# The first batch's convolution taps moved into the attention, half of them to GpSimd, and the last result copies to ScalarE

## The chip, the cores and the metric

The kernel runs on one core of a Trainium2 chip. The metric is the device time of one execution in microseconds. The engines are named as the profile names them: PE is TensorE (PEld its weight loads), DVE is VectorE, ACT is ScalarE, POOL is GpSimd, SP is SyncE, which here only issues DMAs. Each engine works through its own instructions in order and waits on semaphores for the others.

## What is computed

Three layers follow each other on 8 batches of 576 rows and 512 columns: a linear attention over 8 heads, a gated convolution, and a Fourier mixer with an MLP.

```
def phi(x):
    proj = np.einsum('bhsd,df->bhsf', x, w_phi)
    proj = proj - np.max(np.abs(proj), axis=-1, keepdims=True)
    return np.concatenate([np.exp(proj), np.exp(-proj)], axis=-1)
x = (q_p @ (k_p^T v)) / (q_p @ sum(k_p) + 1e-6)      # q_p, k_p = phi(q), phi(k); heads side by side
...
for k in range(5):                                   # xp: x with four rows of zeros ahead
    gate_pre += conv_w[k][None, None, :] * xp[:, k:k + S, :]
gate = 1.0 / (1.0 + np.exp(-gate_pre))
x = (gate * (x @ w_val)) @ w_out
...
u = x + real(fft(fft(x, axis=1), axis=2))
un = (u - mean(u)) / sqrt(var(u) + 1e-06)
out = u + maximum(un @ w_ch1, 0) @ w_ch2
```

The change touches the five products and their sum in `gate_pre`, here called taps, for the first batch, and the way in which the attention's result x gets to memory.

## The kernel before

**The attention** runs in 48 steps (and one more to drain), written out by hand in `run_attention`. A unit is two heads of two batches, and three steps make a unit, so the first two batches are done after the first 12 steps and their way through the pipeline. In a step TensorE does, in this order, the numerators (`emit_num`, tile nm), the key-value sums (`emit_KV`, kv), the transpose of a result (`emit_XT`, xt), the transpose of the projected queries (`emit_yT`, yt) and the two projections of the next step (`emit_P`, pj). In the steps whose number 3 divides, kv is split in two, ahead of nm and behind it. VectorE does in a step twice an absolute maximum and a subtraction on a projection (`emit_Y`, tiles m and y), then the copy of the transposed result out of PSUM (`emit_xT`, tile xT), then the scaling of the next result (`emit_X`, tiles r and xs). The transposed result lies in the PSUM bank of the first projection (pj0), so the next step's projection starts only when xT has been copied. ScalarE does the exponentials (ke, qe). SyncE stores xT to x_scr, the attention's result in DRAM, and loads what is needed.

Beside this, ScalarE and GpSimd turn the weights, which come as 64-bit numbers, into pairs of 32-bit ones, in pieces (`convert`, lines 118 to 156): one TENSOR_SCALAR (L143) and three TENSOR_TENSORs (L144, L149, L150) of 1,024 columns each on GpSimd. The pieces are spread over the attention's steps. Tables are loaded and rounded on the way too (`put_table`).

**The mixer and the MLP** are recorded as operations (`op`) with the keys that they read and write, and a planner (`place_ops`) sets their order on all engines by durations and due times. It also chooses between VectorE and GpSimd where an operation allows both (for instance `o_lo`, the low half of a split), and takes it that two operations with both operands in SBUF don't run on these two at once.

For each batch b and each of four blocks m of 128 channels, `note_taps` makes the gate: the fifth product on ScalarE (an activation with a scale), four SCALAR_TENSOR_TENSORs on VectorE that each multiply by a weight and add, and a sigmoid on ScalarE. The running sum lies in a PSUM bank (pa), but for the first two blocks of the first batch in SBUF (sg). `note_V` is the product with w_val (val) and its multiplication with the gate (gv, val, gs), `note_W` the product with w_out (ps). Before the product the batch is split in a high and a low half (xh): for the first batch in the attention's last steps (`split_x`), for the others by `note_x`.

The first batch's rows are loaded (`load_x`) in step 43 (X_AT), into one of two buffers xf, and the four taps of its first block are put into the steps 46 and 47 (`tap_steps`). The other twelve are the planner's, together with the last steps of the attention that are left over (`note_tail`). The layer norm, much later, uses a buffer A of four blocks and a row of sums s1, in a pool of their own (ln).

Of the kernel before, what the change touches and what calls it, by code (L numbers as in the profile page):

```python
# [9 lines left out]
F32 = mybir.dt.float32  # L10
# [6 lines left out]
ALU = mybir.AluOpType  # L17
# [50 lines left out]
def attention_moe_mixer_kernel(  # L68
# [128 lines left out]
    X_AT = TOT - 5  # L197
    att = ExitStack()
# [7 lines left out]
    late["s1"] = ln_p.tile([128, HB], F32, name="s1")  # L206
    late["A"] = ln_p.tile([128, 4, HB], F32, name="A")
# [19 lines left out]
    wp = ap1.tile([128, F], F32, name="wp")  # L227

# [119 lines left out]
    def emit_xT(i):  # L348
# [60 lines left out]
    def put_table(dst, src):  # L409
        r, n = src.shape  # L410
        t = stg.tile([128, 580], F32, tag="tab", name="tab")
        nc.sync.dma_start(out=t[0:r, 0:n], in_=src)
        yield
        hi_act(dst, t[0:r, 0:n])
        yield
# [60 lines left out]
    def load_x(b):  # L476
        t = P["xf"].tile([128, 4, S + 4], F32, tag="xf", name="xf")
        late["xf", b] = t
        nc.vector.memset(t[:, :, 0:4], 0.0)
        nc.sync.dma_start(out=t[:, :, 4:], in_=x_scr[b].rearrange("c p s -> p c s"))  # L480

    def split_x(c):
# [4 lines left out]
        x = late["xf", 0][:, c, 4:]  # L487
# [6 lines left out]
    def tap_steps():  # L494
        t, acc = late["xf", 0], late["sg", 0]
        act.activation(out=acc, in_=shifted(t, 0, 4), func=ACTF.Copy, scale=cw[:, 0, 4:5])
        for k in range(4):
            vec.scalar_tensor_tensor(
                out=acc, in0=shifted(t, 0, k), scalar=cw[:, 0, k:k + 1], in1=acc, op0=ALU.mult, op1=ALU.add
            )  # L500
            yield
# [12 lines left out]
    def note_taps(b, m):  # L514
        t, s = later(("xf", b % 2)), later(("sg", m % 2))
        xk, sk = ("xf", b % 2), ("sg", m % 2)
        first = b == 0 and m < 2
        acc, k = (s, sk) if first else (later("pa")[:, :, 0:HS], "pa")
        if b or m:
# [776 lines left out]
    def note_tail():  # L1296
# [16 lines left out]
        def xt(i):  # L1313
            op("m", 0, lambda e: emit_XT(i, ps_tr, "tr"), [("xs", i % 3), "att"], ["tr"], CH * 0.11)
            op("v", 0, lambda e: emit_xT(i), ["tr"], [("xT", i % 2)], 0.13 + 0.13 * CH)
# [15 lines left out]
    def run_attention():  # L1331
        lead = ((0, 1), (1, 0), (2, 1), (3, 0), (3, 1), (5, 0), (5, 1))
        todo = {}
        tap0 = tap_steps()
# [5 lines left out]
        with tc.manual_schedule():  # L1340
            for st in range(TOT + 1):
# [43 lines left out]
                for _ in range(2 * (TOT - 2 <= st < TOT)):  # L1385
                    next(tap0)
# [3 lines left out]
                if st == X_AT:  # L1390
                    assert did_t == n_t
                    load_x(0)
                    load_x(1)
                    for i in range(2):
                        late["sg", i] = P["g"].tile([128, 2, HS], F32, tag="acc", name="acc")
# [123 lines left out]
```

## Time and profile before

| | us |
|---|---|
| median of 3 runs | 1322.32 (1319.93 to 1325.2) |
| profiled execution, its own time | 1319.91 |
| span of the profiled execution | 1317.9 |
| TensorE busy | 1285.6 |
| VectorE busy | 1150.3 |
| ScalarE busy | 909.0 |
| GpSimd busy | 771.7 |

The busy times are those of the whole span, in which stages with different limits follow each other. A wait is read from the timeline: behind a row stands in brackets how long its engine had been idle before it, and what ended that. Several instructions of a kind that follow each other stand in one row with their count.

### The profile page before, as it was taken

To read this page: it belongs to the slowest core of one execution; us is meant where nothing else is said; L and a number is where in the kernel's file an instruction comes from. 1 tells how busy PE (TensorE), PEld (TensorE's weight loads), DVE (VectorE), ACT (ScalarE), POOL (GpSimd) and SP (SyncE) were. 2 spreads that over 40 slices of the span, in tenths; PEclk is the share of its full clock that TensorE was granted. 3 is DMA by queue.
4 is the path that set the end of the run, shared out by engine and by line. 5 is a ranking of instruction groups with operands and counts; after the bars stand their busy time and mean duration, and the time that the engine had idled before them with its cause. 6 is when DMAs were issued, how large, how long until landed. Compare 5 with 4: busy or idle time off the path is not lost.

```text
span 1317.9 us, 30729 instructions
## 1 busy us (share of the span) xinstructions
PE 1285.6 (98%) x11952; PEld 1183.4 (90%) x11952; DVE 1150.3 (87%) x1790; ACT 909.0 (69%) x1698; POOL 771.7 (59%) x641
## 2 busy tenths in 40 slices
PE   8999999988999998999999999999999999999998
PEld 7899999977999998998888888888888888889997
DVE  6888888879999999789989989998989888888885
ACT  6888898654556646466867687767677676776662
POOL 4877778224567576264655755596558856583321
PEclk9999999999999999999999999999999999999999
DMA  8689999624343442428433753357333733355322
GB/s 307 205 282 302 297 302 298 193 73 141 117 165 104 165 153 100 146 79 284 132 103 98 227 155 103 104 159 217 105 103 119 238 122 100 104 153 177 105 85 89
DMA packets 147005, 214.62 MB, mean 163 GB/s; under 512 B 18854, under 2 KB 105382, under 8 KB 146860
## 3 DMA queue, kind: packets, MB, share of 16 engines
q1 hardware_dynamic: 142400, 203.06, 47.9%
q10 hardware_dynamic: 4460, 9.62, 2.0%
q8 instruction: 93, 1.52, 0.5%
q14 instruction: 52, 0.43, 0.1%
HBM read 165.63 MB, written 46.99 MB: 161 GB/s over the span
## 4 chain that ended last, share of the span: by engine, by line
PE 89%; DVE 5%; ACT 3%; DMA 1%; issue 1%; SPq 0%; POOL 0%; DVEq 0%; POOLq 0%
PE cx L64 15%; PE x L64 15%; PE ps L64 13%; PE cy L64 11%; PE y L64 8%; PE val L64 7%; PE kv L64 5%; PE pj L64 5%; PE nm L64 4%; PE z L64 4%; PE yt L307 2%; PE xt L345 1%; DVE acc L64 1%; ACT qe L64 1%; DMA r<-s_scr 1%
## 5 line engine op out<-in xcount | busy, mean ns | idle before, releaser
L64 POOL TENSOR_TENSOR r<-r 128x256 fp32r<-128x256 f32 (+1 forms) x301 | 292.7, 989 | 246.5 <-ACT r L64 233.3
L64 ACT ACTIVATE r<-r 128x256 fp32r<-128x256 f32 (+1 forms) x420 | 195.3, 487 | 54.9 <-DMA r<-s_scr 49.9
L64 PE MATMUL x<-un,r 128*128 128x462 f32 (+1 forms) x960 | 221.7, 372 | 2.2 <-ACT c L64 1.4
L64 PE MATMUL cx<-h,r 128*128 128x462 f32 (+1 forms) x960 | 213.9, 371 | 1.1 <-DVE acc L64 1.1
L64 PEld LDWEIGHTS x<-un,r 128*128 128x128 f32 x960 | 180.3, 188 | 23.9 <-DVE c L64 2.0
L64 PEld LDWEIGHTS cx<-h,r 128*128 128x128 f32 x960 | 180.3, 188 | 22.1 <-DVE acc L64 1.9
L64 PE MATMUL cy<-h,r 128*128 128x462 f32 (+1 forms) x720 | 160.2, 371 | 0.0
L64 PEld LDWEIGHTS cy<-h,r 128*128 128x128 f32 x720 | 135.4, 188 | 15.3
L64 PE MATMUL val<-xh,wv 128*128 128x290 f32 x768 | 117.1, 301 | 7.5 <-DVE gs L64 3.8
L64 PEld LDWEIGHTS val<-xh,wv 128*128 128x128 f32 x768 | 107.8, 191 | 10.2 <-DVE gs L64 4.5
L64 PE MATMUL y<-un,r 128*128 128x462 f32 (+1 forms) x480 | 113.9, 372 | 0.7 <-DVE h L64 0.6
L64 DVE SCALAR_TENSOR_TENSOR acc<-xf,cw,acc 128x576 f32<-128x576 f32 x128 | 105.9, 830 | 6.9 <-ACT acc L64 5.9
L64 PE MATMUL ps<-ge,wo 128*128 128x290 f32 x768 | 107.9, 297 | 2.0 <-DVE A L64 1.8
L64 PEld LDWEIGHTS ps<-ge,wo 128*128 128x128 f32 x768 | 104.6, 189 | 2.6 <-DVE A L64 2.1
L266 DVE TENSOR_REDUCE m<-pj 128x6 f32<-128x768 f32 x96 | 91.5, 953 | 15.6 <-PE pj L64 14.2
L64 PEld LDWEIGHTS y<-un,r 128*128 128x128 f32 x480 | 90.0, 188 | 11.9 <-DVE h L64 1.5
L64 DVE TENSOR_TENSOR acc<-cx,acc 128x924 f32<-128x924 f32 (+1 forms) x80 | 89.0, 1112 | 12.6 <-PE cx L64 10.5
L267 DVE TENSOR_TENSOR y<-pj,m 128x768 f32<-128x768 f32 x96 | 92.0, 958 | 6.4
L64 ACT ACTIVATE qe<-yt 128x768 f32<-128x768 f32 x96 | 72.5, 808 | 27.4 <-PE yt L307 27.4
L64 PE MATMUL kv<-vraw,ke 128*64 128x66 f32 x2560 | 88.3, 224 | 1.9 <-ACT kvT L64 1.8
L64 PE MATMUL pj<-wp,kqraw 64*128 64x128 f32 x1152 | 81.9, 290 | 6.9 <-DMA kqraw<-in_k_dram 4.8
L64 PEld LDWEIGHTS pj<-wp,kqraw 64*128 64x128 f32 x1152 | 71.9, 196 | 18.2 <-DVE xT L64 11.1
(170 smaller groups left out, 2719.3 us busy)
## 6 DMA issues: line engine op xcount, KB each, us to landing
r<-s_scr SPq DMA_DIRECT2D x280, 128.0 KB, 2.3
r<-s_scr SPq DMA_DIRECT2D x140, 256.0 KB, 2.6
raw<-in_w_ch_dram SPq DMA_DIRECT2D x32, 512.0 KB, 6.1
vraw<-in_v_dram SPq DMA_DIRECT2D x32, 330.0 KB, 5.7
xf<-x_scr SPq DMA_DIRECT2D x8, 1152.0 KB, 6.7
u_scr<-u ACTq DMA_DIRECT2D x8, 1152.0 KB, 5.3
kqraw<-in_k_dram SPq DMA_DIRECT2D x46, 192.0 KB, 3.7
kqraw<-in_q_dram SPq DMA_DIRECT2D x46, 192.0 KB, 4.0
```

Source lines behind the costliest of these rows:

```text
L64: return lambda *a, **k: f(*(resolve(x) for x in a), **{n: resolve(x) for n, x in k.items()})
L266: nc.vector.tensor_reduce(out=m, in_=pv, axis=AX.X, op=ALU.max, apply_absolute_value=True)
L267: nc.vector.tensor_tensor(out=y, in0=pv, in1=m.unsqueeze(3).to_broadcast([128, 2, CH, F]), op=ALU.subtract)
L307: nc.tensor.transpose(t[:, h, j * F:(j + 1) * F], y[:, h, j, :], ident)
L345: nc.tensor.transpose(t[:, 0, j * F:(j + 1) * F], x[:, j].rearrange("p h d -> p (h d)"), ident)
```

## The change

The fifth product and the four others of all four blocks of the first batch are now done in the attention. The rows of the first batch are loaded in step 19 instead of 43, into a buffer of its own, x0, which lies where the layer norm's A and s1 lie (these are now views of x0). Both xf buffers stay free for the batches that follow.

GpSimd makes the fifth product of all four blocks (`tap_start`, two blocks at the end of step 20, two at the end of step 28) and, for the blocks 0 and 1, the other taps in halves of 288 columns, as a product and a sum (`tap_steps_pool`): eight pairs between the steps 21 and 35, eight in the steps 42 to 45. VectorE makes the four taps each of the blocks 2 and 3 (`tap_steps_dve`), one in each of the steps 21, 24, 27 to 42, with the sum in a new SBUF tile tp. The taps of the steps 46 and 47, and the first batch's in the planner's part, are gone; only the sigmoids are left there.

The copies xT run on ScalarE from step 42 on and in the part that is left over (eleven of 48). The tables are staged in a tile of another pool.

```
+    x0 = ln_p.tile([128, 4, S + 4], F32, name="x0")
+    late["A"] = flat0[:, 0:4 * HB].rearrange("p (c s) -> p c s", s=HB)
+    late["s1"] = flat0[:, 4 * HB:5 * HB]
...
+    tp = ap1.tile([128, 2, 2, HS], F32, name="tp")
...
-        vec.tensor_copy(out=xT[i], in_=t[:, 0, 0:CH * F])
+        (hi_dve if e == "v" else hi_act)(xT[i], t[:, 0, 0:CH * F])
...
+    def tap_start(m):
+        acc = late["sg", m] if m < 2 else tp[:, m - 2]
+        gps.tensor_scalar(out=acc, in0=shifted(x0, m, 4), scalar1=cw[:, m, 4:5], scalar2=None, op0=ALU.mult)
+
+    def tap_steps_pool():
+        for m in range(2):
+            acc = late["sg", m]
+            for k in range(4):
+                for a in range(2):
+                    t = P["g"].tile([128, NE], F32, tag="gv", name="tap")[:, 0:HS]
+                    gps.tensor_scalar(out=t, in0=shifted(x0, m, k)[:, a], scalar1=cw[:, m, k:k + 1], scalar2=None, op0=ALU.mult)
+                    gps.tensor_tensor(out=acc[:, a], in0=acc[:, a], in1=t, op=ALU.add)
+                    yield
+
+    def tap_steps_dve():
+        for m in range(2, 4):
+            acc = tp[:, m - 2]
+            for k in range(4):
+                vec.scalar_tensor_tensor(
+                    out=acc, in0=shifted(x0, m, k), scalar=cw[:, m, k:k + 1], in1=acc, op0=ALU.mult, op1=ALU.add
+                )
+                yield
...
+            op("a", 128 * CH, lambda e: emit_xT(i, "a"), ["tr"], [("xT", i % 2)])
...
+                if X_FIRST + 2 <= st <= X_FIRST + 23 and st % NG == 0:
+                    next(tap_d)
                 if at(5):
                     emit_XT(st - 5, ps_pj, "pj0")
-                    emit_xT(st - 5)
+                    emit_xT(st - 5, "v" if st < X_AT - 1 else "a")
...
-                for _ in range(2 * (TOT - 2 <= st < TOT)):
-                    next(tap0)
+                if st == X_FIRST:
...
+                    load_x(0)
+                for i in range(2):
+                    if st == X_FIRST + 1 + 8 * i:
+                        tap_start(i)
+                        tap_start(i + 2)
+                if X_FIRST + 2 <= st < X_FIRST + 18 and (st - X_FIRST) % 2 == 0:
+                    next(tap_p)
+                if X_AT - 1 <= st < X_AT + 3:
+                    next(tap_p)
+                    next(tap_p)
```

What stands on VectorE in step 21, from the second projection on. Before (m and y are the maximum and the subtraction, xT the copy of the result, r and xs its scaling):

```order
L266 TENSOR_REDUCE m<-pj 128x6
L267 TENSOR_TENSOR y<-pj,m 128x768
L64 COPY xT<-xt 128x384
L335 TENSOR_SCALAR r<-nm 128x6
L336 RECIPROCAL r<-r 128x6
L337 TENSOR_TENSOR xs<-nm,r 128x384
```

And now (x_114 is x0):

```order
L270 TENSOR_REDUCE m<-pj 128x6
L271 TENSOR_TENSOR y<-pj,m 128x768
L64 SCALAR_TENSOR_TENSOR tp<-x_114,cw,tp 128x576
L64 COPY xT<-xt 128x384
L339 TENSOR_SCALAR r<-nm 128x6
L340 RECIPROCAL r<-r 128x6
L341 TENSOR_TENSOR xs<-nm,r 128x384
```

The tap stands between the subtraction and the copy; so it does in the six other steps 24 to 39.

What stands on GpSimd around the end of step 20. Before (mt is the piece of weights in the making, raw its 64-bit numbers, cv a temporary):

```order
L143 TENSOR_SCALAR mt<-raw_2066 128x1024
L144 TENSOR_TENSOR mt<-mt,cv 128x1024
L149 TENSOR_TENSOR mt<-mt,raw_2066 128x1024
L150 TENSOR_TENSOR mt<-mt,cv 128x1024
L143 TENSOR_SCALAR mt<-raw_2176 128x1024
```

And now (acc is the sum of block 0, tp that of block 2, cw the convolution's weights):

```order
L143 TENSOR_SCALAR mt<-raw_2066 128x1024
L144 TENSOR_TENSOR mt<-mt,cv 128x1024
L64 TENSOR_SCALAR acc<-x_114,cw 128x576
L64 TENSOR_SCALAR tp<-x_114,cw 128x576
L149 TENSOR_TENSOR mt<-mt,raw_2066 128x1024
L150 TENSOR_TENSOR mt<-mt,cv 128x1024
L143 TENSOR_SCALAR mt<-raw_2176 128x1024
L144 TENSOR_TENSOR mt<-mt,cv 128x1024
L64 TENSOR_SCALAR tap<-x_114,cw 128x288
L64 TENSOR_TENSOR acc<-acc,tap 128x288
```

The two first products stand behind the second of the four instructions of a piece, and the first pair of halves behind the second instruction of the next piece.

What stands on VectorE where the attention ends, from the scaling of step 46 on. Before:

```order
L337 TENSOR_TENSOR xs<-nm,r 128x384
L64 SCALAR_TENSOR_TENSOR acc<-xf,cw,acc 128x576 x2
L266 TENSOR_REDUCE m<-pj 128x6
L267 TENSOR_TENSOR y<-pj,m 128x768
L266 TENSOR_REDUCE m<-pj 128x6
L267 TENSOR_TENSOR y<-pj,m 128x768
L64 COPY xT<-xt 128x384
L335 TENSOR_SCALAR r<-nm 128x6
```

And now, to the first gate of the first batch (val is the product with w_val):

```order
L341 TENSOR_TENSOR xs<-nm,r 128x384
L270 TENSOR_REDUCE m<-pj 128x6
L271 TENSOR_TENSOR y<-pj,m 128x768
L339 TENSOR_SCALAR r<-nm 128x6
L340 RECIPROCAL r<-r 128x6
L341 TENSOR_TENSOR xs<-nm,r 128x384
L64 SCALAR_TENSOR_TENSOR acc<-xf,cw,acc 128x2x288 x4
L64 TENSOR_TENSOR gv<-val_5453,acc 128x290
L64 TENSOR_TENSOR val_5456<-val_5456,acc 128x290
```

Taps and copies are out of these steps; the four taps ahead of the first gate are those of the second batch.

## Rows read from the trace of the kernel before

**Rows 1.** The page: busy time, share of the span, instructions of each engine.

```profile
PE 1285.6 (98%) x11952; PEld 1183.4 (90%) x11952; DVE 1150.3 (87%) x1790; ACT 909.0 (69%) x1698; POOL 771.7 (59%) x641
```

**Rows 2.** By stage: window, length, busy PE PEld DVE ACT POOL, clock, DMA, GB/s.

```profile
100.00:120.00 20.00, 20.00 (x488) 18.66 (x485) 17.79 (x27) 17.98 (x23) 16.45 (x9) 1.00 0.89 290
273.00:296.00 23.00, 17.94 (x351) 16.41 (x348) 16.89 (x26) 11.68 (x19) 4.11 (x4) 0.93 0.16 51
296.00:330.00 34.00, 28.95 (x306) 27.22 (x306) 32.10 (x63) 14.86 (x22) 14.40 (x20) 0.95 0.41 137
488.00:510.00 22.00, 16.92 (x120) 15.94 (x119) 20.05 (x36) 13.16 (x24) 10.99 (x11) 1.00 0.28 102
```

**Rows 3.** Timeline, TensorE in steps 46 and 47: start, us, engine, line, what, idle before.

```profile
274.35 1.61 PE L64 MATMUL pj<-wp,kqraw 64*128 64x128 f32 x24
...
281.31 0.52 PE L345 MATMUL xt<-ident,xs 128*128 128x128 f32 x3 [2.40 <-DVE y L267]
...
283.54 2.93 PE L64 MATMUL pj<-wp,kqraw 64*128 64x128 f32 x24 [1.05 <-DVE xT L64]
```

**Rows 4.** Timeline, TensorE's waits for VectorE in the first batch.

```profile
301.24 1.87 PE L64 MATMUL val<-xh,wv 128*128 128x290 f32 x12 [1.04 <-DVE gv L64]
309.83 1.62 PE L64 MATMUL nm<-kvT,qe 128*64 128x65 f32 x48 [1.08 <-DVE xs L337]
316.16 1.87 PE L64 MATMUL val<-xh,wv 128*128 128x290 f32 x12 [0.95 <-DVE gs L64]
321.13 4.56 PE L64 MATMUL val<-xh,wv 128*128 128x290 f32 x20 [1.22 <-DVE xh L64]
```

**Rows 5.** Timeline, step 21 and the load that stands ahead of it.

```profile
118.86 0.52 SPq L412 DMA_DIRECT2D tab<-in_feat_tab_dram  x1
...
124.89 2.39 POOL L144 TENSOR_TENSOR mt<-mt,cv 128x1024 int32<-128x1024 int32 x1
...
124.98 0.96 DVE L267 TENSOR_TENSOR y<-pj,m 128x768 f32<-128x768 f32 x1
...
126.62 0.56 DVE L64 COPY xT<-xt 128x384 f32<-128x384 f32 x1 [0.68 <-PE xt L345]
...
127.23 0.86 PEld L64 LDWEIGHTS pj<-wp,kqraw 64*128 64x128 f32 x14 [0.23 <-DVE xT L64]
...
127.36 2.40 POOL L149 TENSOR_TENSOR mt<-mt,raw 128x1024 int32<-128x1024 int32 x1
```

**Rows 6.** Timeline, taps on VectorE beside GpSimd: sum in SBUF, then in PSUM.

```profile
277.21 1.48 POOL L64 TENSOR_TENSOR xh<-xf,xh 128x576 fp32r<-128x576 f32 x1 [3.55 <-ACT xh L64]
...
277.45 1.86 DVE L64 SCALAR_TENSOR_TENSOR acc<-xf,cw,acc 128x576 f32<-128x576 f32 x1
...
305.91 3.21 POOL L64 TENSOR_TENSOR ws<-ws 128x256 f32<-128x256 f32 x4 [6.43 <-DMA ws<-s_scr]
...
306.37 0.82 DVE L64 SCALAR_TENSOR_TENSOR acc<-xf,cw,acc 128x576 f32<-128x576 f32 x1
```

**Rows 7.** Groups on GpSimd, 20 to 262 us: count, busy us, mean ns, idle before.

```profile
L149 POOL TENSOR_TENSOR mt<-mt,raw 128x1024 int32<-128x1024 int32 x20 | 48.4, 2419 | 6.7 <-ACT raw L146 5.9
...
L143 POOL TENSOR_SCALAR mt<-raw 128x1024 int32<-128x1024 uint16 x19 | 22.3, 1174 | 26.0 <-DMA s_scr<-mt 22.0 <-DMA x_scr<-xT 2.5 <-DMA raw<-in_w_ch_dram 1.0
```

**Rows 8.** Timeline, subtractions and running conversions in the steps 27 and 39.

```profile
160.57 0.96 DVE L267 TENSOR_TENSOR y<-pj,m 128x768 f32<-128x768 f32 x1
...
160.61 2.37 POOL L150 TENSOR_TENSOR mt<-mt,cv 128x1024 int32<-128x1024 int32 x1
...
230.16 2.38 POOL L144 TENSOR_TENSOR mt<-mt,cv 128x1024 int32<-128x1024 int32 x1
...
230.97 0.96 DVE L267 TENSOR_TENSOR y<-pj,m 128x768 f32<-128x768 f32 x1
```

**Rows 9.** The page, DMA issues: KB each, us to landing.

```profile
xf<-x_scr SPq DMA_DIRECT2D x8, 1152.0 KB, 6.7
```

**Rows 10.** Timeline, TensorE behind its longest wait in the mixer.

```profile
506.85 1.87 PE L64 MATMUL val<-xh,wv 128*128 128x290 f32 x12 [2.89 <-DVE gs L64]
```

More of the change, by code (lines that the diff above doesn't have):

```diff
@@ L205, in attention_moe_mixer_kernel @@
     ln_p = pool(lx, "ln", 1, side=R)
-    late["s1"] = ln_p.tile([128, HB], F32, name="s1")
-    late["A"] = ln_p.tile([128, 4, HB], F32, name="A")
+    x0 = ln_p.tile([128, 4, S + 4], F32, name="x0")
+    flat0 = x0.rearrange("p c s -> p (c s)")
+    late["A"] = flat0[:, 0:4 * HB].rearrange("p (c s) -> p c s", s=HB)
+    late["s1"] = flat0[:, 4 * HB:5 * HB]
     wv_p = pool(gx, "wv", 1, side=R)
@@ L410, in put_table @@
         r, n = src.shape
-        t = stg.tile([128, 580], F32, tag="tab", name="tab")
+        t = P["g"].tile([128, 2, NE], F32, tag="gs", name="tab").rearrange("p a b -> p (a b)")
         nc.sync.dma_start(out=t[0:r, 0:n], in_=src)
@@ L476, in load_x @@
     def load_x(b):
-        t = P["xf"].tile([128, 4, S + 4], F32, tag="xf", name="xf")
-        late["xf", b] = t
-        nc.vector.memset(t[:, :, 0:4], 0.0)
+        t = late["xf", b] if b else x0
         nc.sync.dma_start(out=t[:, :, 4:], in_=x_scr[b].rearrange("c p s -> p c s"))
@@ L486, in split_x @@
         h, l = late["xh", 0], late["xh", 1]
-        x = late["xf", 0][:, c, 4:]
+        x = x0[:, c, 4:]
         hi_act(h[:, c], x)
@@ L492, in shifted @@
         return t[:, m, k:k + S].rearrange("p (a s) -> p a s", a=2)
[L494 to L501, printed above, removed]
+    def tap_start(m):
[18 more added lines that the diff above has]
+                yield
     def note_x(b):
@@ L516, in note_taps @@
         xk, sk = ("xf", b % 2), ("sg", m % 2)
-        first = b == 0 and m < 2
-        acc, k = (s, sk) if first else (later("pa")[:, :, 0:HS], "pa")
-        if b or m:
+        if b:
+            acc, k = later("pa")[:, :, 0:HS], "pa"
+        else:
+            acc, k = (s, sk) if m < 2 else (tp[:, m - 2], "att")
+        if b:
             o_act(acc, shifted(t, m, 4), ACTF.Copy, 685, [xk], [k], scale=cw[:, m, 4:5])
@@ L1384, in run_attention @@
                     next(c)
-                for _ in range(2 * (TOT - 2 <= st < TOT)):
-                    next(tap0)
+                if st == X_FIRST:
+                    for i in range(2):
+                        late["sg", i] = P["g"].tile([128, 2, HS], F32, tag="acc", name="acc")
+                    nc.vector.memset(x0[:, :, 0:4], 0.0)
+                    load_x(0)
+                for i in range(2):
+                    if st == X_FIRST + 1 + 8 * i:
[6 more added lines that the diff above has]
+                    next(tap_p)
                 while did_t < n_t and did_t * (X_AT - 5) < (st - 3) * n_t:
@@ L1391, in run_attention @@
                     assert did_t == n_t
-                    load_x(0)
+                    for b in range(2):
+                        late["xf", b] = P["xf"].tile([128, 4, S + 4], F32, tag="xf", name="xf")
+                        nc.vector.memset(late["xf", b][:, :, 0:4], 0.0)
                     load_x(1)
-                    for i in range(2):
-                        late["sg", i] = P["g"].tile([128, 2, HS], F32, tag="acc", name="acc")
                 if st in (X_AT + 2, X_AT + 3):
```

6 lines of the change are left out of this document (3 added, 3 removed).

## The prediction

> **What bounds the kernel now.** I read the busy shares first: TensorE is busy for 98% of the span, so only its idle or slowed stretches can be won [rows 1]. The table by stage shows where these are [rows 2]. In the attention TensorE is full (20.00 of 20), VectorE has 17.79 and GpSimd 16.45. From 273 to 330, where the attention hands over to the first batch of the mixer, TensorE loses 5.06 us (23 - 17.94) and then 5.05 us (34 - 28.95), with a granted clock of 0.93 and 0.95, while VectorE has 32.10 of 34 in the second part. A second hole lies at 488 to 510 (22 - 16.92 = 5.08 us).
>
> The timeline at 277 to 284 names the cause of the first part: TensorE's transpose waits 2.40 us for VectorE, the next projection another 1.05 us, and its 24 matmuls then take 2.93 us against 1.61 two steps before [rows 3]. In front of those VectorE rows stand convolution taps of the first batch. In the second part waits for VectorE of 1.04, 1.08 and 0.95 us, all on gates, row scalings or sums queued among taps, and a last one of 1.22 us for the split of the next batch [rows 4]. The change works on exactly this place: 16 taps at some 0.82 us and eleven copies at 0.56 us leave VectorE there.
>
> The steps that receive the taps are then what to look at. In step 21 (all steps with a number that 3 divides look like it) VectorE finishes the second subtraction at 125.94, sits idle for 0.68 us, copies xT until 127.18, and TensorE's projection starts at 127.23, as soon as xT is out of its bank [rows 5]. So in a TensorE that is full, the copy xT is on the path with no slack behind it, and what VectorE has in front of it is 0.68 us (0.77 with the overlap of the two instructions).
>
> **The change part by part.**
>
> Eight taps on VectorE in the attention. Each is put between that subtraction and xT [rows 5]. A tap needs 0.82 us, 0.73 until the next may start, so without any hindrance it just fits into the gap: about 0.05 us a tap. But it reads two operands from SBUF, and so do the conversions of GpSimd. At 277.45 such a tap took 1.86 us: GpSimd's split had begun at 277.21 and ended at 278.69, and the tap's own work came behind that. With its sum in PSUM a tap at 306.37 took 0.82 beside a GpSimd busy with sums of the weights from 305.91 to 309.12 [rows 6]. The new sums (tp) lie in SBUF, so each tap waits for what is left of the running conversion. Price: each piece of weights is three TENSOR_TENSORs of 2.4 us, of which rows 7 show one, and a TENSOR_SCALAR of 1.17 us; some 60 and 19 of them in 242 us [rows 7] leave a mean rest of (60 x 2.4 x 2.4 + 19 x 1.17 x 1.17) / (2 x 242) = 0.77 us at a moment of no relation to them. At the six places where the taps 2 to 7 go, the trace of before has for instance 1.5 us left in step 27 (160.61 + 2.37 against 161.53 less the overlap of 0.09) and 0.7 in step 39 [rows 8]. The least is nothing, the most a whole conversion, 2.4 us. I take 0.8 each: six taps, **+5 us**, with 0 and 14 as ends. TensorE has no idle time with which to make this up.
>
> The first tap is dearer. Its sum is begun by GpSimd, and the order puts these two instructions behind the conversion that ends at 127.28 in the trace [rows 5]. They also need the batch's rows: that load is issued where the table load at 118.86 stands [rows 5]; alike loads land after 6.7 us (125.6) [rows 9], and in an attention that moves 290 GB/s [rows 2] the 1.18 MB can take 4.1 us longer (129.6). I take 127.8. Two TENSOR_SCALARs of 576 columns, at most 1.17 us each by the 1,024 columns of rows 7 and 0.66 by their share, 0.7 taken, end at 129.2; the tap ends by 130.0, and xT, before at 126.62, starts 3.4 us late. If the conversion that follows on GpSimd (2.40 us, row at 127.36) begins before the tap does, it is 5.8. No row shows this race; I take 4.6. A TensorE idle so long may lose its clock: 1.32 us were lost behind 2.40 + 1.05 us [rows 3], nothing behind 2.89 us (twelve matmuls in 1.87, as at 316.16) [rows 4, 10]. I count 1.3, so **+6 us**, ends 3.4 and 8.
>
> The eighth tap, in step 42, meets no conversion and no xT on VectorE: nothing.
>
> The other half on GpSimd: 4 first products and 16 pairs of product and sum. By rows 7 a pair costs up to 288/1024 of 1.17 and 2.42, or 1.0 us, some 19 us in all. Eight pairs lie among conversions, which leave GpSimd 3.5 of 20 us [rows 2]; nobody but the stores waits for a conversion at once, and if they came so late that ScalarE waited, its exponentials would. Eight lie behind the last conversion, where GpSimd has nothing. Zero, with that cover.
>
> Here a rule speaks against the change. Beside VectorE's subtraction at 124.98, which reads PSUM, GpSimd's conversion from 124.89 costs it nothing: 0.96 us [rows 5]. The Trainium skill (Perfetto Trace Analysis, Optimizing Scalar/DVE Operations) warns that the two share a read port of SBUF, so that moving work from one to the other may not help. By the row only VectorE's own eight taps meet that port, and the sum below stands; by the rule more of GpSimd's added work comes back as waits of VectorE, and the time would be that of the first rival.
>
> What else moves: the load of the first batch goes past 24 steps of SyncE's queue. The loads behind it land up to 4.1 us later once; the keys and queries of a unit are asked for six steps ahead, and values and weights have a step or more, so nothing; if a piece of weights were late, ScalarE, which reads it first, would stand for some us. The small clearing of x0 on VectorE and the tables' other tile: nothing. A and s1 as views of x0 are first written when the first batch is long done: nothing.
>
> Copies on ScalarE: eleven copies of 384 columns. In the last steps ScalarE waits for the transpose behind it anyway, and the copy takes its place in the same gap; nothing, or up to 0.5 us a copy (0.56 on VectorE, rows 5) if exponentials stand in front of it.
>
> What is won: the whole of 2.40 + 1.05 + 1.32 = 4.8 us at the attention's end [rows 3], since no tap and no copy is left in VectorE's steps there. Of the next 35 us, 1.04 + 1.08 + 0.95 = 3.1 us [rows 4]; the taps of the next batch, four in a row, come before the first gate, where VectorE would be idle. At 321.13 20 matmuls took 4.56 us where 12 take 1.87, 1.4 us too long, behind a wait of 1.22 us [rows 4]. That wait is for splits of the next batch that one buffer holds back, and stays in kind; I count 1.2 of the 2.6. **-9 us**, ends 5 and 11. What is late next is that split.
>
> The rest of the mixer gets another order from the planner, and gives five more splits to VectorE, so that little of its relief is left at 488. I count nothing, and 3 us either way. From the MLP on TensorE's order is as before.
>
> Sum: 5 + 6 - 9 = **+2 us** on a profiled execution of 1319.91 us (its span of 1317.9 and 2.0 around it), which lies 2.4 us under the median of the three runs; on the median, 1322.3 + 2 = **1324 us**.
>
> **The rivals.**
>
> Slower: GpSimd's conversions own VectorE's taps. If the first tap loses the race and the clock (8 us), the six others wait 1.5 us each instead of 0.8 (9 us), and only 7.5 us are won, it is +9.5: **1332 us**. For it speaks that GpSimd gets more work in those steps, so fewer gaps; against it the rests read at the places, which are smaller. It decides from 1.3 us a tap on (8 + 8 - 9 = +7).
>
> Faster: the relief of VectorE reaches the hole at 488 to 510. There a gate's sums came 2.89 us late [rows 10], with VectorE at 20.05 of 22 [rows 2]. If these 5 us go too, the first tap costs 4 and the others 0.5 each, it is 4 + 3 - 9 - 5 = -7: **1315 us**. Against it: TensorE runs ahead by as much as VectorE is relieved.
>
> The change does not do what it says: the first batch is held by the split and by the sigmoids on ScalarE behind a table load, and only the 4.8 us at the attention's end come: 11 - 5 = +6, **1328 us**.
>
> **How the numbers follow.** Chances: the forecast 0.55, slower 0.2, faster 0.15, not done 0.1. A measurement of this kernel can tell about 0.5%, 6.6 us, from no change. The forecast's own range is 1319 to 1330. Of the faster case most lies beyond 6.6 us, and a little of the forecast's lower end; of the slower case most, with a part of the last: faster 0.18, same 0.59, slower 0.23. The range, with a tenth left out on either side, is 1314 to 1333.
>
> **What the profile would show.** Right: in step 21 an idle TensorE of 3 to 6 us ended by xT; in steps 24 to 39 a tap of 0.8 to 3 us and a projection late by as much over 0.7; no wait of TensorE for VectorE at the attention's end; steps there at 5.7 and 6.2 us. Wrong: taps at 0.82 us in all steps (then some 5 us faster), a first tap that finds its sum ready, or waits of TensorE for ScalarE's copies.

## The result, and the profile after

The changed kernel takes 1327.36 us in the median of 7 runs (1324.96 to 1332.06); the kernel before, beside it, 1319.21 us (7 runs). The ratio is 1.0056, 95% interval 1.0034 to 1.0077: slower by some 7 to 8 us. The forecast was +2 us (1324 on a median of 1322.3); the time lies in the range 1314 to 1333, and the difference is 5 to 6 us larger than forecast. The prediction gave 0.59 to no change and 0.23 to a slowdown beyond 6.6 us, the least that it took a measurement to tell; the 7 to 8 us lie just beyond that.

First the page of the changed kernel, busy time, share and instructions of each engine; it answers to [rows 1].

```profile
PE 1286.3 (97%) x11952; PEld 1182.4 (89%) x11952; DVE 1144.8 (86%) x1775; ACT 909.9 (69%) x1705; POOL 802.5 (61%) x674
```

TensorE does the same work in a longer span (1325.4 us in the profiled execution, 1317.9 before). GpSimd has 30.8 us more. Where the time lies shows in the table by stage (window, length, busy PE PEld DVE ACT POOL, clock, DMA, GB/s), beside [rows 2]:

```profile
100.00:120.00 20.00, 20.00 (x472) 18.66 (x467) 17.59 (x29) 17.48 (x22) 16.82 (x9) 1.00 0.90 291
120.00:140.00 20.00, 11.58 (x213) 10.70 (x213) 12.30 (x17) 11.15 (x14) 12.39 (x7) 0.77 0.68 238
287.20:305.20 18.00, 16.40 (x353) 15.05 (x348) 10.48 (x18) 12.04 (x20) 3.51 (x3) 1.00 0.26 80
305.20:340.00 34.80, 32.99 (x347) 31.26 (x346) 29.18 (x61) 18.17 (x30) 12.86 (x14) 1.00 0.31 111
340.00:498.00 158.00, 153.53 (x1137) 149.89 (x1136) 146.40 (x276) 87.54 (x180) 93.70 (x91) 1.00 0.42 143
498.00:520.00 22.00, 20.63 (x154) 20.00 (x154) 20.97 (x39) 15.93 (x36) 14.09 (x14) 1.00 0.32 121
```

One new hole of 8.42 us (20 - 11.58) with a clock of 0.77 stands at 120 to 140. The end of the attention and the first batch now lose 1.60 and 1.81 us at full clock, where 5.06 and 5.05 us were lost. The hole at 488 to 510 has shrunk to 1.37 us, but 4.47 us are lost in the 158 us ahead of it, where the kernel before lost 0.36:

```profile
330.00:488.00 158.00, 157.64 (x1185) 156.36 (x1184) 150.84 (x282) 92.62 (x188) 103.92 (x92) 1.00 0.41 142
```

The waits of TensorE in the changed kernel (120 to 600 us; total, times, longest):

```profile
PE pj L64 <- DVE xT L64: 12.5, 6, 8.4
PE val L64 <- DVE gv L64: 3.6, 5, 1.0
PE yt L311 <- ACT qe L64: 1.6, 1, 1.6
PE ps L64 <- POOL f L64: 1.1, 2, 0.6
PE val L64 <- DVE gs L64: 1.0, 4, 0.4
PE xt L349 <- ACT xT L64: 0.9, 1, 0.9
```

Six waits for xT, one of them 8.4 us long, stand behind the six taps out of eight that a conversion of GpSimd held up. To follow this step by step I compare the start of TensorE's transpose xt in both timelines (us):

| start of | before | after | later by | change since the line above |
|---|---|---|---|---|
| xt, step 21 | 126.04 | 125.37 | -0.67 | -0.67 |
| xt, step 22 | 132.25 | 142.31 | 10.06 | +10.73 (first tap) |
| xt, step 40 | 237.71 | 252.50 | 14.79 | +4.73 (six taps) |
| xt, step 48 | 290.03 | 299.18 | 9.15 | -5.64 (attention's end) |
| the MLP's first product | 596.82 | 604.13 | 7.31 | -1.84 (handover, mixer) |
| end of the span | 1317.94 | 1325.44 | 7.50 | +0.19 |

The timeline of the changed kernel in step 21 shows the first tap; it answers to [rows 5]:

```profile
118.19 0.65 SPq L482 DMA_DIRECT2D x<-x_scr  x1
...
124.04 2.39 POOL L144 TENSOR_TENSOR mt<-mt,cv 128x1024 int32<-128x1024 int32 x1
...
128.08 1.73 POOL L64 TENSOR_SCALAR acc<-x,cw 128x576 f32<-128x576 f32 x1 [1.65 <-DMA x<-x_scr]
129.79 1.73 POOL L64 TENSOR_SCALAR tp<-x,cw 128x576 f32<-128x576 f32 x1
...
131.48 2.38 POOL L149 TENSOR_TENSOR mt<-mt,raw 128x1024 int32<-128x1024 int32 x1
131.55 2.92 DVE L64 SCALAR_TENSOR_TENSOR tp<-x,cw,tp 128x576 f32<-128x576 f32 x1 [6.27 <-POOL tp L64]
...
134.40 0.54 DVE L64 COPY xT<-xt 128x384 f32<-128x384 f32 x1
...
134.99 2.93 PE L64 MATMUL pj<-wp,kqraw 64*128 64x128 f32 x24 [8.42 <-DVE xT L64]
...
137.86 2.87 PE L64 MATMUL nm<-kvT,qe 128*64 128x65 f32 x48
140.51 1.87 PE L64 MATMUL kv<-vraw,ke 128*64 128x66 f32 x48
```

The rows land at 128.08, the two products take 1.73 us each, and the next conversion begins 0.07 us ahead of the tap, which then ends 0.61 us behind it. The copy xT starts 8.45 us late (134.40 against 126.62 - 0.67). The rest is the clock: in the windows 134.99 to 137.86 and 137.86 to 140.70 the granted clock is 0.50, that is 1.2 of 2.4 GHz, and TensorE's next three groups take 2.93, 2.87 and 1.87 us where 1.61, 1.62 and 1.57 are usual, 2.87 us more. Of the 10.73 us only 2.28 are left for it, because in the kernel before this step had itself lost 0.53 us (6.22 us from xt to xt; an undisturbed one takes 5.69).

At the attention's end the rows that answer to [rows 3] and [rows 4] have no wait left above 0.9 us (one of 1.60 us, of the transpose yt for ScalarE's qe, stands in step 48 of both kernels):

```profile
293.05 0.55 PE L349 MATMUL xt<-ident,xs 128*128 128x128 f32 x3
...
294.22 1.61 PE L64 MATMUL pj<-wp,kqraw 64*128 64x128 f32 x24
...
307.76 1.62 PE L64 MATMUL nm<-kvT,qe 128*64 128x65 f32 x48
...
310.94 2.68 PE L64 MATMUL val<-xh,wv 128*128 128x290 f32 x18 [0.35 <-DVE gs L64]
...
325.43 0.55 PE L349 MATMUL xt<-ident,xs 128*128 128x128 f32 x3 [0.89 <-ACT xT L64]
...
327.08 4.71 PE L64 MATMUL val<-xh,wv 128*128 128x290 f32 x30 [0.30 <-DVE gs L64]
```

### The profile page after: what moved, and what is told of

Same layout as the page of the kernel before. It is cut to its first block, busy times and chain, and to the rows that moved or that the text cites. A ratio compares the mean times of both kernels' runs of the same rounds, so it can differ in the third digit from the quotient of the medians.

```text
span 1325.4 us, 30762 instructions
## 1 busy us (share of the span) xinstructions
PE 1286.3 (97%) x11952; PEld 1182.4 (89%) x11952; DVE 1144.8 (86%) x1775; ACT 909.9 (69%) x1705; POOL 802.5 (61%) x674
## 4 chain that ended last, share of the span: by engine, by line
PE 81%; DVE 8%; ACT 5%; DMA 3%; POOL 2%; issue 2%; SPq 0%; DVEq 0%; POOLq 0%; ACTq 0%
PE cx L64 14%; PE x L64 14%; PE cy L64 11%; PE ps L64 10%; PE y L64 8%; PE pj L64 5%; PE val L64 4%; PE kv L64 4%; PE nm L64 4%; PE z L64 4%; DVE acc L64 2%; PE yt L311 2%; PE xt L349 1%; DVE m L270 1%; DMA r<-s_scr 1%
## 5 line engine op out<-in xcount | busy, mean ns | idle before, releaser
L64 DVE SCALAR_TENSOR_TENSOR acc<-xf,cw,acc 128x576 f32<-128x576 f32 x112 | 91.2, 814 | 11.6 <-ACT acc L64 11.0
L64 PE MATMUL pj<-wp,kqraw 64*128 64x128 f32 x1152 | 82.3, 291 | 17.2 <-DVE xT L64 12.5
```

Of the source, the lines that this page charges most:

```text
L64: return lambda *a, **k: f(*(resolve(x) for x in a), **{n: resolve(x) for n, x in k.items()})
```

## The experiments

All times in this table are from the runs; the last five columns are from the one profiled execution of each and say by how much TensorE took longer than in the profiled execution before, in the stretches of the table above.

| kernel | median, us | before, same chip | ratio (95%) | 21 to 22 | 22 to 40 | 40 to 48 | 48 to MLP | MLP |
|---|---|---|---|---|---|---|---|---|
| changed | 1327.36 | 1319.21 | 1.0056 (1.0034 to 1.0077) | 10.73 | 4.73 | -5.64 | -1.84 | 0.2 |
| e1_late3 | 1320.52 | 1322.10 | 0.9987 (0.9971 to 1.0003) | -0.53 | 7.80 | -5.64 | -1.62 | 1.4 |
| e7_first | 1324.52 | 1320.35 | 1.0018 (1.0000 to 1.0036) | 5.02 | 4.61 | -5.64 | -0.93 | 3.2 |
| e2_psum | 1316.58 | 1322.10 | 0.9958 (0.9942 to 0.9973) | -0.53 | 3.98 | -5.64 | -0.78 | -0.5 |
| e3_act_xT | 1319.05 | 1322.10 | 0.9977 (0.9959 to 0.9996) | -0.53 | 3.52 | -5.59 | -1.59 | 0.2 |
| e10_vector_half | 1319.11 | 1321.18 | 0.9983 (0.9967 to 0.9999) | 0.20 | 4.28 | -5.64 | -2.33 | -0.2 |
| e4_no_taps | 1314.09 | 1322.10 | 0.9939 (0.9916 to 0.9962) | -0.53 | 2.50 | -5.64 | -1.79 | -0.4 |
| e11_no_taps2 | 1314.53 | 1321.45 | 0.9952 (0.9938 to 0.9967) | -0.20 | 1.24 | -5.64 | -1.48 | 3.4 |
| e9_gpsimd_half | 1317.12 | 1321.18 | 0.9968 (0.9950 to 0.9986) | -0.53 | 2.70 | -5.64 | -1.32 | -0.3 |
| e12_gpsimd2 | 1316.52 | 1321.45 | 0.9966 (0.9951 to 0.9981) | -0.53 | 3.12 | -5.64 | -2.02 | 4.1 |
| e8_late_load | 1315.34 | 1320.35 | 0.9948 (0.9929 to 0.9967) | -0.07 | 1.08 | -5.60 | -1.56 | 1.3 |
| e6_copies | 1319.16 | 1320.35 | 0.9984 (0.9967 to 1.0001) | -0.53 | 1.19 | -1.51 | -0.34 | 0.8 |
| e5_end | 1315.49 | 1320.35 | 0.9956 (0.9939 to 0.9973) | 0.29 | 1.07 | -5.64 | -1.50 | 3.9 |

Some columns need a caution. In the first, -0.53 is an undisturbed step, since the kernel before lost 0.53 us there. e6_copies does in the steps 21 to 40 what the kernel before does, and still shows 1.19 there; e5_end and e8_late_load show 1.1 too. So some 1.1 us in that column is an execution's own; e4_no_taps, without any tap, shows 2.50. And the MLP, which no edit touches, differs by up to 4 us from one execution to the other, so what the trace alone shows is worth that much, and I go by the medians first. The profiled execution is also not always a middle one: that of e9_gpsimd_half is its fastest (1313.25 us), that of e5_end its slowest (1318.73).

The kernel before took 1319.21 us beside the changed kernel and 1320.35 to 1322.10 beside the others. Most times named in the expectations are on the former, so kernels of different chips are compared by their ratios.

**The first tap.** e1_late3 takes it away, e7_first makes it cheaper.

```diff
-                if X_FIRST + 2 <= st <= X_FIRST + 23 and st % NG == 0:
+                if X_FIRST + 5 <= st <= X_FIRST + 26 and st % NG == 0:
                     next(tap_d)
```

> The changed kernel with VectorE's eight taps one unit later (steps 24 to 45 in place of 21 to 42), nothing else moved. Six of them still stand ahead of the copy xT, in the same six steps; only the tap whose sum GpSimd has just begun is gone. Theory: in the changed kernel this first tap alone cost TensorE 10.7 us (8.4 us of waiting and 2.3 us at a lower clock), and nothing gives it back, so 1327.4 - 10.7 = 1316.7 us (1315 to 1319), with TensorE's start of step 22 where it was before the change. Rival: the stall belongs to the early load and to GpSimd's own delay, and comes again at another wait: 1324 to 1328.

Against the changed kernel the ratio falls by 0.0069, 9.1 us. The median of 1320.52 us lies over the theory's 1315 to 1319, but the kernel before is 2.9 us slower there too, and by the ratio the time is 1317.5 on the first measurement's before. The delay of step 22 is gone, whole, and doesn't come again: the theory holds, and with it goes more than the whole loss. By itself the kernel is at most 0.3% from before (the interval holds 1). Its steps 24 to 39 were dearer than the changed kernel's, since other taps met other conversions and TensorE once waited for kvT; both are taken up below.

```diff
-                if st == X_FIRST:
+                if st == X_FIRST - 2:
                     nc.vector.memset(x0[:, :, 0:4], 0.0)
                     load_x(0)
...
-                        tap_start(i)
                         tap_start(i + 2)
+                        tap_start(i)
```

> The changed kernel with the first tap made cheaper, nothing else moved: the load of the first batch in step 17 in place of 19, and GpSimd begins block 2, which VectorE needs, ahead of block 0 (and block 3 ahead of block 1). Theory: the delay of TensorE at step 22, 10.7 us, was 1.65 us for the load, 1.73 us for each of two first products, 2.2 us for the tap that lost against the next conversion, 2.3 us of slow clock, and the step's own. Now the load is there, one product stands in front of the tap, and the instruction that gets in ahead of it is a product of 1.73 us in place of 2.38: a delay of 5.5 to 7 us, and a time 3.5 to 5 us under the changed kernel's. Rival: the tap finds its operands only when the conversion behind is over as well, so that only the load is won: 1.7 us.

Step 22 is 5.02 us late in place of 10.73, and the ratio lies 0.0038 (5.0 us) under the changed kernel's. The tap waits for one product only, and no conversion gets in ahead of it, but the product of block 0: it takes 1.30 us. The slow clock is still there behind a wait of 4.04 us (24 matmuls in 2.93 us), but the next 48 take 1.80 where they took 2.87. The delay is 0.5 us under the theory's 5.5 to 7, the time at the end of its 3.5 to 5, so the parts are right to about that much.

**The six taps behind it.** e2_psum takes away the second operand in SBUF, e3_act_xT the copy behind the tap, e10_vector_half GpSimd's added work; the first two stand on e1_late3.

```diff
+        late["pj"] = pv.rearrange("p h c f -> p h (c f)")[:, :, 0:HS]
...
-                    out=acc, in0=shifted(x0, m, k), scalar=cw[:, m, k:k + 1], in1=acc, op0=ALU.mult, op1=ALU.add
+                    out=acc, in0=shifted(x0, m, k), scalar=cw[:, m, k:k + 1], in1=late["pj"], op0=ALU.mult, op1=ALU.add
```

> As e1_late3, but each of VectorE's taps reads as its second operand a piece of the projection in PSUM that it has just subtracted, in place of the running sum in SBUF (the sum of blocks 2 and 3 is left out). Number, place and size of the instructions stay. Theory (a VectorE instruction with two operands in SBUF waits for GpSimd's running conversion): taps of 0.82 us, the six steps 24 to 39 lose at most 0.3 us in place of 4.7, so e1_late3 less 4.5 us, about 1312. Rival (the tap's own length ahead of xT is what costs): TensorE's delay over the six steps stays at 3 to 5 us, and the time is that of e1_late3.

A tap beside a conversion in the timeline of e1_late3:

```profile
235.03 2.37 POOL L144 TENSOR_TENSOR mt<-mt,cv 128x1024 int32<-128x1024 int32 x1
235.09 2.94 DVE L64 SCALAR_TENSOR_TENSOR tp<-x,cw,tp 128x576 f32<-128x576 f32 x1
...
237.49 2.79 POOL L149 TENSOR_TENSOR mt<-mt,raw 128x1024 int32<-128x1024 int32 x1
...
238.55 2.68 PE L64 MATMUL pj<-wp,kqraw 64*128 64x128 f32 x24 [2.08 <-DVE xT L64]
```

And one beside the same kind of conversion in the timeline of e2_psum:

```profile
217.37 2.41 POOL L149 TENSOR_TENSOR mt<-mt,raw 128x1024 int32<-128x1024 int32 x1
218.10 0.80 DVE L64 SCALAR_TENSOR_TENSOR tp<-x,cw,pj 128x576 f32<-128x576 f32 x1
```

All eight taps of e2_psum take 0.80 or 0.81 us, and no wait for xT is left; the time falls by 0.0029 (3.8 us). In e1_late3 two taps of 2.80 and 2.94 us began 0.17 and 0.06 us after a conversion had begun and cost 1.95 and 3.65 us, the second with the clock. That a tap with two operands in SBUF waits for GpSimd is shown. The Trainium skill (SBUF — State Buffer, "Who interferes with whom") says it in the same way: a VectorE instruction with two inputs in SBUF contends with a GpSimd instruction that reads SBUF, because its second input comes through a read interface that the two share, and the shared pair of ports is an exclusive lock. The trace agrees: the tap of 2.94 us ends 0.62 us behind the conversion. That the six steps would lose at most 0.3 us did not hold: e2_psum still loses 3.7 us in the steps 32 to 34, by another wait, of TensorE for kvT, told with GpSimd's half.

```diff
-                    emit_xT(st - 5, "v" if st < X_AT - 1 else "a")
+                    emit_xT(st - 5, "v" if st < X_AT - 1 and not (st >= X_FIRST + 5 and st % NG == 0) else "a")
```

> As e1_late3, but in the six steps 24 to 39 with a tap the copy xT runs on ScalarE, so that no tap stands ahead of it. Theory (a tap costs because it is ahead of xT, whatever makes it long): the six steps cost at most 1 us in place of 4.7, so about 1312 to 1314. Rival: ScalarE stands in an activation of 1.2 us of the conversions when the transposes end, so that xT starts up to 1.2 us late there, 4 to 7 us over six steps: 1316 to 1319.

By the trace the theory holds: taps of 1.29 and 1.66 us stand there without a wait of TensorE for VectorE, and 22 to 40 fell from 7.80 to 3.52. What is left is one wait for kvT (1.2) and two of 0.69 us for ScalarE's xT, in the steps 24 and 33; there ScalarE stands in an activation of 1.26 and 1.23 us of the conversions, the rival's cause, but in two steps of six. By the medians the kernel is only 0.0010 (1.3 us) under e1_late3, within the spread, and its 1319.05 us, or 1316.2 on the first before, is nearer to the rival's 1316 to 1319 than to the theory's 1312 to 1314. So the medians don't decide, and how much of these 4 us is to be had in every execution stays open.

```diff
-        gps.tensor_scalar(out=acc, in0=shifted(x0, m, 4), scalar1=cw[:, m, 4:5], scalar2=None, op0=ALU.mult)
+        act.activation(out=acc, in_=shifted(x0, m, 4), func=ACTF.Copy, scale=cw[:, m, 4:5])
...
-                        tap_start(i)
                         tap_start(i + 2)
...
-                    next(tap_p)
+                    pass
```

> The changed kernel with VectorE's half alone: the first products of blocks 2 and 3 on ScalarE, the load in step 17 so that they needn't wait, nothing of the convolution on GpSimd (the products and sums of blocks 0 and 1 are left out). VectorE's taps stay in steps 21 to 42, ahead of xT. Theory: a tap ends 0.62 us behind the conversion that runs when it starts and costs nothing where none runs; seven such places with a mean rest of 0.8 us cost 4 to 7 us over e4_no_taps: 1317 to 1321, and step 22 no more than 3 us late. Rival: with GpSimd less busy the taps meet no conversion, and the time is that of e4_no_taps.

The ratio is 0.0031 over that of e11_no_taps2 and 0.0044 over that of e4_no_taps, 4 to 6 us, as the theory has it. Five of its taps met a conversion (1.59, 2.19, 1.73, 1.99, 1.65 us), three did not (0.81), and the first, which found its sum ready, cost no more than the others: step 22 is 0.20 late, 0.73 against an undisturbed step.

**What the added work costs elsewhere.** e4_no_taps and e11_no_taps2 (one kernel) leave out all of it, e9_gpsimd_half and e12_gpsimd2 (one kernel) leave out VectorE's taps only, e8_late_load moves the load.

```diff
-                    next(tap_d)
+                    pass
...
-                        tap_start(i)
-                        tap_start(i + 2)
+                        pass
...
-                    next(tap_p)
+                    pass
```

> The changed kernel without the first batch's taps: no products and sums on GpSimd and none on VectorE in the attention (the gate of the first batch is taken from its rows alone, all five products are left out); the order of everything else is the same. It shows what the change wins when its new work is free. Theory: the work costs 10.7 + 4.7 us on VectorE and nothing on GpSimd, so 1327.4 - 15.4 = 1312 us. Rival: GpSimd's half costs too, through conversions that come later, and the time is under 1309.

> e4_no_taps once more, beside e12_gpsimd2 on one chip: no taps of the first batch. It is the lower end for what follows; 0.5 to 0.7% under before by either theory.

Twice 0.5 to 0.6% under before: what the change wins is 6 to 8 us, and the new work takes all of it and as much again (0.0117, 15 us between e4_no_taps and the changed kernel; the changed trace has 10.73 + 4.73).

The edit of e9_gpsimd_half and e12_gpsimd2 is the first of these three alone.

> The changed kernel without VectorE's eight taps (of blocks 2 and 3 only the first product is left, the other four are left out); GpSimd does all that it does in the changed kernel. Theory (the prediction's price of GpSimd's half: nothing): as e4_no_taps, 0.6% under before, about 1312 to 1315. Rival (GpSimd's added products make the pieces of weights late, the next piece's load with them, and ScalarE, which reads it first, stands ahead of the copies and exponentials that TensorE needs, as e1_late3 and e2_psum showed in step 33): 2 to 4 us over e4_no_taps, TensorE waiting for kvT in one or two steps.

> e9_gpsimd_half once more, beside e11_no_taps2 on one chip: GpSimd's half alone. Its traces show no more lost time than those without taps, its median lay 0.3% over theirs. Theory (GpSimd's half costs nothing): within 1.5 us of e11_no_taps2. Rival (it makes pieces of weights late in some executions): 2 to 5 us over it.

e9_gpsimd_half is 0.32% under before where its theory has 0.6%; it lies 0.0029 (3.8 us) over e4_no_taps, measured on another chip, in its rival's range, with an uncertainty of about 0.003. e12_gpsimd2 lies 0.0014 (1.9 us) over e11_no_taps2, between its theory and its rival. By the ratios, which each bring in the spread of the kernel before, the uncertainty is 0.002 and doesn't exclude zero. Compared directly, on one chip, the medians are 1.99 us apart, and eight of the twelve runs of e11_no_taps2 are faster than the fastest of e12_gpsimd2; resampling the runs gives 0.8 to 3.2 us (95%). The trace has a place for this price, in step 33 of e12_gpsimd2:

```profile
194.21 1.57 PE L64 MATMUL nm<-kvT,qe 128*64 128x65 f32 x48
...
195.29 1.15 ACT L142 ACTIVATE cv<-raw 128x1024 int32<-128x1024 uint32 x1 [2.05 <-DMA raw<-in_w_ch_dram]
196.35 0.38 ACT L64 ACTIVATE kvT<-kv 128x260 f32<-128x260 f32 x1
...
196.78 1.15 PE L64 MATMUL kv<-vraw,ke 128*64 128x66 f32 x32 [0.99 <-ACT kvT L64]
```

ScalarE waits 2.05 us for a piece of weights, and the copy kvT, which TensorE needs, stands behind it in its queue. TensorE's wait for kvT in step 33 is 0.99 us here, 1.10 in e1_late3, 1.98 in e2_psum, 1.17 in e3_act_xT and 0.60 in e9_gpsimd_half: in all five kernels that have GpSimd's half and no stall in step 21, ScalarE stands idle for 1.03 to 2.41 us ahead of this piece. What ended this idle time is the piece's load in three of them, a conversion of GpSimd in e3_act_xT and not shown in e9_gpsimd_half. In none of the kernels without GpSimd's added work in these steps does ScalarE wait there. So GpSimd's half has a price of some 2 us, and the late pieces are shown; that these make up all of the price is not shown. In the changed kernel and in e7_first no such wait stands in step 33; that their own stalls of 8.4 and 4 us gave the pieces time is likely, and not tested.

```diff
                 if st == X_FIRST:
...
-                    load_x(0)
...
                 if st == X_AT:
...
+                    load_x(0)
                     load_x(1)
```

> As e4_no_taps (no taps of the first batch, all five products left out), with the load of the first batch in step 43, where it stood before the change, in place of 19. Theory: the load of 1,152 KB in a part of the attention in which the DMA engines are busy for over 90% makes other loads late, and the waits of TensorE in steps 24 and 27 (1.9 us together) are its price: they go, and the time is 1 to 2 us under e4_no_taps. Rival: these waits come of something else (the tables' new tile, the order): same as e4_no_taps within 0.7 us.

In the trace the wait of step 27 is 0.15 us in place of 1.25 and the one before step 24, 0.73 us, is gone, but the ratios agree (0.9948 and 0.9939), and e11_no_taps2, with the early load, has no wait in step 27 at all and one of 0.61 us before step 24. A price of the load is not shown; it can't be more than 1 or 2 us, and stays open.

**What is won.** e6_copies is the kernel before with the copies on ScalarE.

```diff
-        vec.tensor_copy(out=xT[i], in_=t[:, 0, 0:CH * F])
+        (hi_dve if e == "v" else hi_act)(xT[i], t[:, 0, 0:CH * F])
...
-                    emit_xT(st - 5)
+                    emit_xT(st - 5, "v" if st < X_AT - 1 else "a")
```

> The kernel before with one part of the change alone: the last eleven copies xT on ScalarE; all taps of the first batch stay where they were before (four in steps 46 and 47, twelve in the planner's part). Theory: of the 4.8 us lost at the attention's end the wait of 2.40 us stays (it is behind two taps, not behind a copy), the 1.05 us and the slow matmuls behind it (1.32) go, and little changes later: 1.5 to 3 us under before. Rival: the copies alone free VectorE enough for the whole of it, 5 us or more under before; or nothing, since the taps are in front anyway.

1.51 us are won by step 48 of the 5.64, and the wait for y behind the two taps stays (2.43 us at 281.15). The wait of 1.05 us went, as the theory had it. The slow clock did not: granted 0.50 between 281.15 and 283.00, the groups behind that wait take 0.87, 1.49 and 2.19 us where 0.55, 0.82 and 1.61 are usual. With 0.0016 (2 us) under before, and an interval that reaches 1, the time fits the theory's 1.5 to 3 us. The larger part of the gain, 4.1 of the 5.64 us, is by difference the taps' leaving these steps; no run takes the taps alone away. The clock has a share in it: in the kernel before the granted clock is 0.50 (1.2 of 2.4 GHz) from 283.47 to 286.88 and again from 321.02 to 324.43, which is the part of the time "too long" that the prediction read at 321.13; in the changed kernel the clock is 1.00 from 141.14 to the mixer's end.

**Another place for the same work.** e5_end puts all of it behind the conversions.

```diff
-    X_FIRST = 19
+    X_FIRST = 38
...
-        gps.tensor_scalar(out=acc, in0=shifted(x0, m, 4), scalar1=cw[:, m, 4:5], scalar2=None, op0=ALU.mult)
+        act.activation(out=acc, in_=shifted(x0, m, 4), func=ACTF.Copy, scale=cw[:, m, 4:5])
...
-                if X_FIRST + 2 <= st <= X_FIRST + 23 and st % NG == 0:
+                if st >= X_AT:
                     next(tap_d)
...
-                    if st == X_FIRST + 1 + 8 * i:
+                    if st == X_AT - 2 + i:
...
+                if X_AT - 1 <= st < X_AT + 5:
+                    for _ in range(3 if st < X_AT + 3 else 2):
+                        next(tap_p)
+                if st == TOT:
+                    next(tap_d)
+                    next(tap_d)
```

> The changed kernel with all of the first batch's work behind the conversions: the load in step 38 in place of 19, the four first products on ScalarE at the ends of steps 41 and 42, VectorE's taps one each in steps 43 to 47 and three in step 48 (there the copies xT are ScalarE's already), GpSimd's sixteen pairs in steps 42 to 47. Order of everything else as in the changed kernel. Theory (VectorE's taps cost because they meet conversions ahead of xT; the gain is that of VectorE's relief at the end): steps 21 to 40 as before the change, and in the last steps VectorE has 0.8 to 1.4 us of idle time in each, so the time is that of the kernel without these taps, 0.6% under before (1312 to 1314 by a before of 1320). Rival: taps and GpSimd's products with both operands in SBUF hold each other up in the last steps, by up to 1.0 us each, and TensorE waits there: 4 to 6 us more, 1317 to 1319.

The ratio is 0.9956, 5.8 us under the kernel before and some 13 us under the changed one. It is 0.5 and 2.2 us over the two measurements of the kernel that leaves the work out, which is within their uncertainty; the median of 1315.49 us lies 1.5 us over the theory's 1312 to 1314 and under the rival's 1317. The longest of its eight taps takes 1.20 us, and TensorE has no wait for VectorE in the attention's last steps. The idle time of VectorE that the change made there is enough for all of its taps.

## Why the prediction came out too low

What bounds the kernel, and the places where the change works, were read rightly: TensorE's waits for xT in the steps with a tap are 12.5 us, the clock comes on top, and nearly all of the gain lies behind step 44. The size of the first tap was wrong. That the time still lies in the range is in part luck: the range is 19 us wide, and the forecast of 1324 stood on a median of 1322.3 us, 3.1 above the one that the changed kernel was measured beside. The terms:

- **First tap, +6: mis-sized, 10.73 measured.** Even the upper end of 8 was too low. Of the 3.85 us by which xT came later than taken, 2.06 are the two products: 0.7 us each was taken, between bounds from another form of TENSOR_SCALAR [rows 7], 16-bit numbers and constants; with a weight per partition and 32-bit numbers one takes 1.73. 1.2 us are the race, which I left at the middle and which was lost. The load took 9.89 us from its issue to landing (118.19 to 128.08) where 8.94 was taken (118.86 to 127.8), 0.95 more; in the steps between 0.36 us less was needed. The clock cost 2.28 in place of 1.3, or 2.87 by the rows. This one term is 4.7 of the 5.5 us of the error.
- **Six taps, +5: held**, 4.73, of which about 1.1 may be an execution's own; five of them have a wait of TensorE for xT behind them, 4.1 us together. They found 0, 1.40, 0.65, 0.96, 1.67 and 1.12 us left of GpSimd's instruction, a mean of 0.97 where 0.77 was taken. With other luck the same six places cost more (e1_late3).
- **Eighth tap, 0: held** (0.81 us, nothing late).
- **GpSimd's half, 0: no cost seen in the changed kernel's trace, but not free by itself.** A pair takes 1.0 + 0.8 us, not 1.0, and the new work is 36.5 us, not 19 (6.9 for the first products, 29.6 for the pairs); GpSimd's busy time grows by 30.8, since five splits of the mixer left it. Without the first tap's stall a piece of weights is late for ScalarE, which the prediction had named and ruled out, and TensorE waits 0.60 to 1.98 us in step 33; the medians put the price of GpSimd's half alone at 2 us.
- **Load, tables, copies on ScalarE, 0: held**; one copy made TensorE wait, 0.89 us at 325.43, a sign that the prediction had listed as wrong. A price of the early load of 1 or 2 us is not excluded. ScalarE's copy takes 0.49 us, right behind the transposes.
- **Gain, -9: 7.5 measured.** The attention's end gave 5.64 where 4.8 was counted, in every kernel without the taps there. Handover and mixer gave 1.84 where 4.3 and 0 ± 3 were counted: the waits of [rows 4] went and the hole of [rows 10] shrank, but from 340 us on five waits for the gate's first product (gv, 3.6 us; 0.5 in three before) came in their place. Why they came is read from the traces alone, and no run tests it.
- **The rivals.** The slower one was right on the first tap (race and clock lost, "8 us", even too low) and on the gain ("only 7.5 us are won"), wrong on the six taps, which cost 0.8 us each and not 1.5; with +9.5 it comes nearer to the 7.5 us than the forecast's +2. That the last one names 1328 us, next to the measured time, is chance: its 11 us of loss were 15.5, and more was won than the 5 us that it left. The rule of the Trainium skill (Perfetto Trace Analysis, Optimizing Scalar/DVE Operations), that the shared read port may eat what is won by moving work between these two, is borne out by VectorE's own taps. What GpSimd's share costs, as far as the traces show it, came back through ScalarE, and not as waits of VectorE.
- **What the profile would show.** The idle TensorE of step 21 was 8.42 us, not 3 to 6. The taps of 0.8 to 3 us (0.81 to 2.29), the missing waits for VectorE at the attention's end and the steps of 5.7 and 6.2 us there came as said.

The sum with the measured sizes is -0.67 + 10.73 + 4.73 - 5.64 - 1.84 + 0.19 = 7.5 us.

## What to carry to other kernels

A price for an instruction has to come from a row of its own form, with the same types and the same kind of scalar; columns alone gave 0.7 us for 1.73. Where a VectorE instruction with two operands in SBUF stands in front of what the bounding engine waits for, count the rest of GpSimd's running instruction, and put no instruction there whose operand the other engine has only just begun to make. Work that a change takes off a stage leaves idle time in that stage: look there first for a place to put it.

## What the runs showed of the hardware

- Whether VectorE's tap is held up goes by the form of GpSimd's instruction. In the six kernels with these taps, in all 24 meetings with a TENSOR_TENSOR or the conversions' 16-bit TENSOR_SCALAR of which more than 0.25 us was left, the tap ended 0.61 or 0.62 us behind that instruction. In 8 of 9 such meetings with a 32-bit TENSOR_SCALAR that has a weight per partition it took its 0.81 to 0.83 us; the ninth, 1.30 us, is the first tap of e7_first. That one began 0.05 us behind the beginning of GpSimd's product, the eight others 0.29 us or more, so the first moments of such a product are not covered by the eight. One from e3_act_xT:

```profile
179.25 1.74 POOL L64 TENSOR_SCALAR acc<-x,cw 128x576 f32<-128x576 f32 x1
180.02 0.81 DVE L64 SCALAR_TENSOR_TENSOR tp<-x,cw,tp 128x576 f32<-128x576 f32 x1
```

The Trainium skill (SBUF — State Buffer, "Who interferes with whom") counts every GpSimd instruction that reads SBUF; by these rows this form, which reads SBUF, does not hold VectorE up. The other way round it does wait: begun 0.02 us behind a tap, such a product took 1.58 us in place of 1.00 (e5_end):

```profile
257.48 0.81 DVE L64 SCALAR_TENSOR_TENSOR tp<-x,cw,tp 128x576 f32<-128x576 f32 x1
257.50 1.58 POOL L64 TENSOR_SCALAR tap<-x,cw 128x288 f32<-128x288 f32 x1
```

- GpSimd pays too: a TENSOR_TENSOR of a conversion that begins some 0.5 us before a held tap ends takes 2.75 to 2.81 us, where 2.36 to 2.43 are usual. In e10_vector_half one began only 0.06 us before the tap's end, and took 2.40.
- TensorE's clock fell also behind stalls far shorter than the first tap's. Behind 2.08 us (e1_late3) its next two groups took 2.68 and 2.12 us, where 1.61 and 1.62 are usual, at a granted clock of 0.56 and 0.77; behind 4.04 us (e7_first) 2.93 and 1.80 at 0.50 and 0.96; behind 8.42 us (the changed kernel) 2.93 and 2.87, both at 0.50, that is 1.2 of 2.4 GHz. Each clock is that of the group's window. Behind 1.94 us, in step 36 of e1_late3, and behind the 2.89 us of [rows 10] the next group took its usual time.
